# Reordering the end of a step: the next layer norm's logarithm and exponential after the last chunk's reciprocals, and two of chunk 6's normalisation products after chunk 7's mask product

## The chip, the cores and the metric

The kernel runs on one core of a Trainium2 chip, in one launch. The metric is the device time of that launch in microseconds (us), the median of several runs. A core has five engines with an instruction queue each: TensorE (PE, the matrix products; its weight loads are shown as PEld), VectorE (DVE), ScalarE (ACT), GpSimd (POOL) and SyncE (SP, which here only issues the weight transfers).

## The reference, cut to what matters

Four residual blocks, A, B, A, B, on x of 2048 rows by 640 columns, each of the form x + block(layernorm(x)):

```python
def A(x, mem0, Wq, Wk, Wv, Wo):            # 32 heads of 192
    mem = mem0                             # 8 rows
    for s in range(64):                    # segments of 32 rows, one after the other
        h = concat([mem, x[32*s:32*s+32]]) # 40 rows
        q, k, v = h @ Wq, h @ Wk, h @ Wv
        p = softmax(mask(q @ k.T * 192**-0.5))
        o = (p @ v) @ Wo
        mem, out[s] = o[:8], o[8:]

def B(x, wqkv, wo):                        # 32 heads of 20
    # each row attends to 8 earlier rows, 2 apart (itself included)
    return softmax(q @ k_window.T * 20**-0.5) @ v_window @ wo
```

The layer norm is (x - mean) / sqrt(variance + 1e-5), without weights. The memory of A makes its segments a chain. The weights are the same in both A blocks and in both B blocks.

## The kernel before, in words

**Two lanes.** The first A block and the second A block run side by side as two lanes, lane 1 being 3 segments (LAG) behind lane 0: a step t handles segment t in lane 0 and segment t - 3 in lane 1. There are 64 + 3 = 67 steps with A work. In steps 3 to 63 both lanes are full (61 steps, 80 columns: 2 lanes of 8 memory rows and 32 segment rows); in steps 0 to 2 and 64 to 66 only one lane is (40 columns). Block B of a segment runs one and two steps later, cut into pieces that stand between the pieces of A.

**Chunks.** The 32 heads of A are cut into 8 chunks of 4 heads. A chunk has: the projections k, q (`proj`, L220, 30 products each) and v (L249, 10 products); the scores `a_s` (8 products, L267 and L268, into the PSUM tile ps_s; then the exponential E on ScalarE, L270, and its product with a 0/1 mask on VectorE, Em, L273); `a_pv` (8 products of Em with Vt into ps_o, L286; a column block of ones in Vt gives the softmax sums; ScalarE takes their reciprocal R as exp(-ln(sum)): four logarithms, L290, one exponential, L292); `a_norm` (three VectorE products of ps_o with R into OT: L300 for the first and third block of each head pair on all 128 partitions, L301 and L302 for the shared middle block, on partitions 0 to 63 and on 64 to 127); and `a_o` (30 products of OT with Wo, L313, summed over all chunks in ps_acc). `a_o` begins with the 20 products that read what L300 wrote; the last 10 read what L301 and L302 wrote.

**Buffers.** ps_o is two PSUM banks with one buffer (`ps_two`, bufs=1), shared by all chunks: `a_pv` of a chunk may begin once `a_norm` of the chunk before has read ps_o. R, E, Em and QT have one buffer each, OT has two. Four single banks (`ps_big`) go round for the projections, the statistics of the layer norm (ps_st) and block B.

**Weights.** The 64 half-chunks of Wk, Wq, Wv, Wo (480 KB each) are read once per step. 34 of them stay in SBUF; the other 30 go through a ring of 6 buffers (w_ring, L190), each loaded by SP as soon as PE has finished with the buffer.

**Order.** The whole step is under a manual schedule: on each engine the instructions stand in the order in which `step` calls for them, and an engine works its queue in that order, waiting at an instruction until the semaphores that it needs are there.

**The end of a step**, in the order of the code before:

1. `a_k(7)`, `a_q(7)`, `ln1_sq` (square of the next segment's x, L331), `a_pv` of chunk 6, v of chunk 7 and its copies to Vt (L258).
2. `a_norm(6)`: L300, L301, L302 on VectorE.
3. `a_s` of chunk 7: 8 products, E on ScalarE, Em on VectorE. Then `a_o(5)`: 30 products.
4. `ln1(nt)`, the next segment's layer norm: 10 products with ones into ps_st (L339); on VectorE the mean (L346), its square (L348), the variance ln_v (L349); on ScalarE a logarithm (L350) and an exponential (L352), which give 1/sqrt; on VectorE x - mean (L358, which does not read ScalarE's result).
5. `a_pv` of chunk 7 (8 products; four L290 and one L292 on ScalarE), `a_norm(7)` on VectorE, `a_o(6)`: 30 products.
6. `ln1_apply`: two VectorE products (L364) that write the scaled rows to hT.
7. `b_v` and `b_k` of block B: 25 and 30 products (L393) and the ScalarE copies VTB (L410) and KB (L399).
8. `a_o(7)`: 30 products. Then `mem_out` (L327: the memory rows from ps_acc to hT), `b_x1` (L374), `b_q` (30 products) and `b_vt` (5 transposes).

The next step then begins with `a_k(0)`, which reads hT.

Of the kernel before, what the change touches and what calls it, by code (L numbers as in the profile page):

```python
# [60 lines left out]
class Kernel:  # L61
# [230 lines left out]
        nc.scalar.activation(out=rf, in_=rf, func=ACT.Exp, scale=-1.0)  # L292
        self.ov, self.r = ov, r

    def a_norm(self, i):
        nc = self.nc
        ov, r = self.cols(self.ov), self.cols(self.r[:])
        ot = self.ap2.tile([P, 2, 3, NT], BF16, name="OT")
        oc = self.cols(ot[:])
        nc.vector.tensor_tensor(out=oc[:, :, 0:3:2], in0=ov[:, :, 0:4:3], in1=r, op=ALU.mult)  # L300
        nc.vector.tensor_tensor(out=oc[0:64, :, 1], in0=ov[0:64, :, 1], in1=r[0:64, :, 0], op=ALU.mult)  # L301
        nc.vector.tensor_tensor(out=oc[64:P, :, 1], in0=ov[64:P, :, 2], in1=r[64:P, :, 1], op=ALU.mult)  # L302
        self.ots[i] = ot

    def a_o(self, i):
        nc = self.nc
# [35 lines left out]
    def ln_small(self, ps):  # L342

        nc = self.nc
        m = self.ap2.tile([P, NX], F32, name="ln_m")
        nc.vector.tensor_scalar(out=m[:], in0=ps[:, 0:NX], scalar1=1.0 / D, scalar2=None, op0=ALU.mult)  # L346
        v = self.bp.tile([P, NX], F32, name="ln_v")
        nc.vector.tensor_tensor(out=v[:], in0=m[:], in1=m[:], op=ALU.mult)  # L348
        nc.vector.scalar_tensor_tensor(out=v[:], in0=ps[:, NX:2 * NX], scalar=1.0 / D, in1=v[:], op0=ALU.mult, op1=ALU.subtract)  # L349
        nc.scalar.activation(out=v[:], in_=v[:], func=ACT.Ln, bias=self.eps_t[:])  # L350
        r = self.ap2.tile([P, NX], F32, name="ln_r")
        nc.scalar.activation(out=r[:], in_=v[:], func=ACT.Exp, scale=-0.5)  # L352
        return m, r
# [24 lines left out]
        self.bsq = self.ln_sq(x1)  # L378

    def b_ln(self, b):  # L380
        self.bmr = self.ln_small(self.ln_stats(self.x1[b], self.bsq))

    def b_ln_apply(self, b):
        dst = self.h2T[:].rearrange("p c (l n) -> p c l n", l=2)
# [110 lines left out]

    def ln1(self, t):
        x = self.xin[t % 2]
        self.amr = self.ln_small(self.ln_stats(x, self.asq))
        self.axc = self.ln_center(x, self.amr)

    def ln1_apply(self, t):
        self.ln_scale(self.axc, self.amr, self.lanes(self.hT[t % 2][:, 0:NC * NT])[:, :, :, NM:LT])
# [1 line left out]
    def prologue(self):  # L504
        nc = self.nc
        self.x1, self.ots, self.qxs, self.ebs = {}, {}, {}, {}
        self.x_load(0)
        nc.sync.dma_start(out=self.m0T[:], in_=self.mem0)
        nc.vector.tensor_copy(out=self.lanes(self.hT[0][:, 0:NC * NT])[:, :, 0, 0:NM], in_=self.m0T[:])
        self.ln1_sq(0)  # L510
        self.ln1(0)
        self.ln1_apply(0)
        self.build_mask_a()

    def step(self, t):
        T = self.n_seg + LAG
        self.set_lanes(t)
        b1 = t - 1 if 0 <= t - 1 < T else None
        b2 = t - 2 if 0 <= t - 2 < T else None
        nt = t + 1  # L520
        a = t < T
        for i in range(NQUAD - 1):
            if a:
                self.a_k(i, t)
                self.a_q(i, t)
                ps = self.a_v(i, t)
                if i >= 1:
                    self.a_pv()
                self.a_v_out(ps)
                if i >= 2:  # L530
                    self.a_o(i - 2)
            if i == 0 and b1 is not None:
                self.b_ln(b1)
            if b2 is not None and 3 <= i <= 4:
                self.b_pv(i - 3)
            if a and i >= 1:
                self.a_norm(i - 1)
            if b2 is not None and i == 6:
                self.b_wo(b2)
            if b2 is not None:  # L540
                if 1 <= i <= 3:
                    self.b_s(b2, 2 * i - 2)
                    self.b_s(b2, 2 * i - 1)
                if i < 3:
                    self.b_qexp(2 * i)
                    self.b_qexp(2 * i + 1)
                if i == 5:
                    self.b_ot()
            if i == 3 and b1 is not None:
                self.b_ln_apply(b1)  # L550
            if a:
                self.a_s()
            if t == 1 and i in (0, 3):
                self.load_b_weights(i)
            if t == 1 and i == 4:
                self.build_masks_b()
            if i == 1:
                if nt < self.n_seg:
                    self.x_load(nt)
                yseg = t - 3 - LAG  # L560
                if yseg >= 0 and yseg % 4 == 3:
                    self.y_store(yseg // 4)
        if a:
            self.a_k(7, t)
            self.a_q(7, t)
        if nt < T:
            self.ln1_sq(nt)
        if a:
            self.a_pv()
            self.a_v_out(self.a_v(7, t))  # L570
            self.a_norm(6)
            self.a_s()
            self.a_o(5)
        if nt < T:
            self.ln1(nt)
        if a:
            self.a_pv()
            self.a_norm(7)
            self.a_o(6)
        if nt < T:  # L580
            self.ln1_apply(nt)
        if b1 is not None:
            self.b_v(b1)
            self.b_k(b1)
        if a:
            self.a_o(7)
            if nt < T:
                self.mem_out(t)
            self.b_x1(t)
        if b1 is not None:  # L590
            self.b_q(b1)
            self.b_vt()
# [78 lines left out]
```

## Time and profile before

| what | value |
|---|---|
| median of 3 runs | 3419.46 us (3419.04 to 3421.05) |
| the profiled execution | 3423.99 us, of which the profile's span is 3422.3 us |
| granted TensorE clock, mean | 0.99 |
| distance between the memory copies (L327) of two full steps | 50.18 us (in most of them) |
| PE, PEld | 3290.0 us busy (96%), 2885.0 us (84%) |
| DVE, ACT, POOL | 64%, 54%, 11% |
| DMA | 299 GB/s on average |

How to read it: shares are of the span. A row of the timeline gives the start in us from the span's start, the duration in us, the engine, the line, the operation, what it writes and reads, how many equal instructions are merged in it, and in brackets how long the engine had been idle before it and what ended that. Matrix products overlap in the pipeline, so a product's duration is a latency; what counts is the distance between starts (some 0.036 us between products of 80 columns). A line of the waits gives the waiting instruction, what released it, the total in us, how often, and the longest. Durations of VectorE and ScalarE instructions overlap a little too, so that sums are made from starts.

### The profile page before, as it was taken

How to read it: one execution, taken by the hardware profiler on the slowest of the kernel's cores; microseconds unless marked ns; L12 is line 12 of the kernel's file. 1: busy time of each engine (PE TensorE's matmuls, PEld its weight loads, DVE VectorE, ACT ScalarE, POOL GpSimd, SP SyncE). 2: the span in 40 equal slices, each digit the busy share in tenths (PEclk: the TensorE clock that was granted, in tenths of full speed). 3: DMA queues.
4: the chain of work that ended last, by engine and by line, in shares of the span. 5: the costliest groups of instructions: out<-in, count | busy, mean ns of one | idle time of the engine just before them, and what ended most of it. 6: DMA issues, size and time to landing. Idle time of an engine off the chain costs nothing.

```text
span 3422.3 us, 164367 instructions
## 1 busy us (share of the span) xinstructions
PE 3290.0 (96%) x72896; PEld 2885.0 (84%) x72896; DVE 2185.0 (64%) x5966; ACT 1843.2 (54%) x5830; POOL 387.9 (11%) x575
## 2 busy tenths in 40 slices
PE   6899999999999999999999999999999999999996
PEld 4788888888888888888888888888888888888875
DVE  2566666666666666666666666666666666666654
ACT  2455555555555555555555555555555555555543
POOL 0210111011011011101101100110110111011011
PEclk8999999999999999999999999999999999999998
DMA  9988888888888888888888888888888888888894
GB/s 393 349 299 295 307 294 293 307 297 294 298 307 295 293 307 293 296 304 298 294 293 307 295 293 308 292 297 300 302 294 297 308 294 293 310 293 297 296 334 153
DMA packets 298410, 1023.85 MB, mean 299 GB/s; under 512 B 34288, under 2 KB 34288, under 8 KB 297568
## 3 DMA queue, kind: packets, MB, share of 16 engines
q1 hardware_dynamic: 294624, 1004.85, 84.6%
q8 instruction: 570, 9.34, 1.1%
q0 software_dynamic: 3072, 8.48, 0.8%
q14 instruction: 144, 1.18, 0.1%
HBM read 1010.58 MB, written 2.62 MB: 296 GB/s over the span
## 4 chain that ended last, share of the span: by engine, by line
PE 85%; DVE 6%; ACT 4%; DMA 3%; issue 1%; POOL 0%; SPq 0%; POOLq 0%; ACTq 0%
PE ps_v L249 25%; PE ps_k L220 16%; PE ps_q L220 16%; PE ps_acc L313 13%; PE ps_o L286 4%; ACT R L290 2%; PE ps_s L267 2%; PE ps_s L268 2%; PE ps_bq L393 2%; PE ps_bs L433 2%; DVE OT L300 2%; PE ps_by L476 1%; DMA w_ring<-in_A_Wv_dram 1%; DVE Vt L258 1%; ACT R L292 1%
## 5 line engine op out<-in xcount | busy, mean ns | idle before, releaser
L290 ACT ACTIVATE R<-ps_o 64x160 f32<-64x160 f32 (+1 forms) x2144 | 625.4, 292 | 823.8 <-issue 517.3
L258 DVE CAST Vt<-ps_v 80x384 bf16<-80x384 f32 x1072 | 557.9, 550 | 407.9 <-PE ps_o L286 335.5
L249 PEld LDWEIGHTS <-hT 128*128 128x128 bf16 x5360 | 495.3, 99 | 296.6 <-issue 15.6
L425 POOL TENSOR_TENSOR QX<-QB,hmask 128x384 bf16<-128x384 bf16 (+1 forms) x402 | 325.6, 829 | 2844.2 <-ACT QB L404 2204.0
L220 PEld LDWEIGHTS <-w_ring 128*128 128x128 bf16 x15075 | 597.1, 100 | 20.3 <-issue 11.5
L249 PE MATMUL ps_v<-w_ring,hT 128*128 128x384 bf16 x2680 | 532.5, 330 | 5.1 <-DMA w_ring<-in_A_Wv_dram 5.1
L249 PE MATMUL ps_v<-w_v,hT 128*128 128x384 bf16 x2680 | 530.3, 329 | 3.3 <-DMA w_v<-in_A_Wv_dram 3.3
L313 PE MATMUL ps_acc<-OT,w_o 128*128 128x80 bf16 (+1 forms) x9045 | 482.3, 200 | 38.1 <-DVE OT L300 35.9
L300 DVE TENSOR_TENSOR OT<-ps_o,R 128x320 bf16<-128x320 f32 (+1 forms) x536 | 254.3, 475 | 374.4 <-ACT R L292 370.4
L238 DVE CAST QT<-ps_q 128x480 bf16<-128x480 f32 (+1 forms) x536 | 340.2, 635 | 228.6 <-PE ps_q L220 207.4
L313 PEld LDWEIGHTS <-w_o 128*128 128x128 bf16 x9045 | 385.6, 99 | 44.6 <-issue 43.4
L220 PE MATMUL ps_q<-hT,w_q 128*128 128x80 bf16 (+1 forms) x9045 | 405.1, 200 | 5.1 <-DMA w_q<-in_A_Wq_dram 5.1
L313 PE MATMUL ps_acc<-OT,w_ring 128*128 128x80 bf16 (+1 forms) x7035 | 400.0, 200 | 1.5 <-DMA w_ring<-in_A_Wo_dram 1.5
L220 PE MATMUL ps_k<-hT,w_ring 128*128 128x80 bf16 (+1 forms) x8040 | 370.1, 200 | 9.3 <-issue 4.2
L220 PE MATMUL ps_k<-hT,w_k 128*128 128x80 bf16 (+1 forms) x8040 | 369.9, 200 | 4.7 <-issue 2.7
L220 PEld LDWEIGHTS <-w_q 128*128 128x128 bf16 x9045 | 351.0, 100 | 6.1 <-DMA w_q<-in_A_Wq_dram 6.0
L220 PE MATMUL ps_q<-hT,w_ring 128*128 128x80 bf16 (+1 forms) x7035 | 324.4, 200 | 7.7 <-issue 3.9
L220 PEld LDWEIGHTS <-w_k 128*128 128x128 bf16 x8040 | 315.8, 100 | 5.5 <-issue 3.0
L231 ACT CAST KF<-ps_k 128x320 bf16<-128x320 f32 (+1 forms) x536 | 219.5, 409 | 164.7 <-PE ps_k L220 164.1
L313 PEld LDWEIGHTS <-w_ring 128*128 128x128 bf16 x7035 | 306.6, 99 | 1.9 <-DMA w_ring<-in_A_Wo_dram 1.8
L286 PEld LDWEIGHTS <-Vt 80*128 80x128 bf16 x4288 | 208.8, 98 | 81.2 <-DVE Em L273 28.2
L286 PE MATMUL ps_o<-Em,Vt 80*128 80x80 bf16 (+1 forms) x4288 | 239.1, 199 | 20.5 <-DVE Em L273 20.5
(94 smaller groups left out, 4058.1 us busy)
## 6 DMA issues: line engine op xcount, KB each, us to landing
w_ring<-in_A_Wk_dram SPq DMA_DIRECT2D x536, 480.0 KB, 5.1
w_ring<-in_A_Wv_dram SPq DMA_DIRECT2D x536, 480.0 KB, 5.0
w_ring<-in_A_Wq_dram SPq DMA_DIRECT2D x469, 480.0 KB, 4.9
w_ring<-in_A_Wo_dram SPq DMA_DIRECT2D x469, 480.0 KB, 5.3
w_q<-in_A_Wq_dram SPq DMA_DIRECT2D x9, 480.0 KB, 9.6
w_o<-in_A_Wo_dram SPq DMA_DIRECT2D x9, 480.0 KB, 9.6
w_k<-in_A_Wk_dram SPq DMA_DIRECT2D x8, 480.0 KB, 9.6
w_v<-in_A_Wv_dram SPq DMA_DIRECT2D x8, 480.0 KB, 9.8
```

Of the source, the lines that this page charges most:

```text
L220: nc.tensor.matmul(ps[:, NT * n + self.c0:NT * n + self.c1], lhsT=w[:, c, P * (n % 3):P * (n % 3 + 1)], rhs=hT[:, NT * c + self.c0:NT * c ...
L231: nc.scalar.copy(out=kf, in_=pv[:, :, 0:3:2, :])
L238: self.nc.vector.tensor_copy(out=self.cols(qt[:]), in_=self.cols(ps[:, 0:6 * NT].rearrange("p (a n) -> p a n", a=6)))
L249: nc.tensor.matmul(ps[:, 0:384], lhsT=hT[:, NT * c:NT * c + P], rhs=w[:, c, :], start=(c == 0), stop=(c == NC - 1))
L258: self.nc.vector.tensor_copy(out=dst, in_=src)
L267: nc.tensor.matmul(self.cols(sv[:, h]), lhsT=kf[:, NT * h:NT * h + P], rhs=self.cols(qt[:, 3 * pr + 2 * j]), start=True, stop=False)
L268: nc.tensor.matmul(self.cols(sv[:, h]), lhsT=kz[:, NT * h:NT * h + P], rhs=self.cols(qt[:, 3 * pr + 1]), start=False, stop=True)
L286: nc.tensor.matmul(self.cols(ov[:, pr, k]), lhsT=vt[0:NT, 512 * pr + c0:512 * pr + c0 + P], rhs=self.cols(em[0:NT, 2 * pr + k // 2]), star ...
L290: nc.scalar.activation(out=self.cols(r[r0:r0 + 64, :, j]), in_=self.cols(src), func=ACT.Ln)
L300: nc.vector.tensor_tensor(out=oc[:, :, 0:3:2], in0=ov[:, :, 0:4:3], in1=r, op=ALU.mult)
L313: nc.tensor.matmul(self.acc[:, NT * c + self.c0:NT * c + self.c1], lhsT=w[m // 3][:, m % 3, P * c:P * (c + 1)], rhs=self.cols(ot[:, m]), s ...
L425: self.nc.gpsimd.tensor_tensor(out=qx[:, 0:nh, :], in0=self.qb[:, c, :].unsqueeze(1).to_broadcast([P, nh, NX]), in1=self.hmask[:, 0:nh, :] ...
```

## The change

Two things move at the end of a step; nothing is added to or taken from the computation, and the instructions of POOL and SP stay as they are.

`ln1` is cut in two. Its products, its VectorE part and x - mean stay where they were; the logarithm and the exponential on ScalarE (L350 and L352) are issued by `ln1_rstd` after `a_pv` of chunk 7, so that on ScalarE they stand behind the four L290 and the L292 of chunk 7 and ahead of the copies VTB and KB. The layer norm of block B (`b_ln`) keeps its order.

`a_norm(6)` is cut in two. L300 stays in its place; L301 and L302 are issued by `a_norm_mid` after `a_s` of chunk 7, so that on VectorE the order is L300, L273 (Em of chunk 7), L301, L302, where it was L300, L301, L302, L273. All other chunks keep their order.

```diff
-    def a_norm(self, i):
+    def a_norm(self, i, split=False):
         ...
+        self.norm = ov, r, oc
         nc.vector.tensor_tensor(out=oc[:, :, 0:3:2], in0=ov[:, :, 0:4:3], in1=r, op=ALU.mult)
+        self.ots[i] = ot
+        if not split:
+            self.a_norm_mid()
+
+    def a_norm_mid(self):
+
+        nc = self.nc
+        ov, r, oc = self.norm
         nc.vector.tensor_tensor(out=oc[0:64, :, 1], in0=ov[0:64, :, 1], in1=r[0:64, :, 0], op=ALU.mult)
         nc.vector.tensor_tensor(out=oc[64:P, :, 1], in0=ov[64:P, :, 2], in1=r[64:P, :, 1], op=ALU.mult)
-        self.ots[i] = ot
...
         nc.vector.scalar_tensor_tensor(out=v[:], in0=ps[:, NX:2 * NX], scalar=1.0 / D, in1=v[:], op0=ALU.mult, op1=ALU.subtract)
+        return m, v
+
+    def ln_rstd(self, m, v):
+        nc = self.nc
         nc.scalar.activation(out=v[:], in_=v[:], func=ACT.Ln, bias=self.eps_t[:])
         r = self.ap2.tile([P, NX], F32, name="ln_r")
         nc.scalar.activation(out=r[:], in_=v[:], func=ACT.Exp, scale=-0.5)
...
     def b_ln(self, b):
-        self.bmr = self.ln_small(self.ln_stats(self.x1[b], self.bsq))
+        self.bmr = self.ln_rstd(*self.ln_small(self.ln_stats(self.x1[b], self.bsq)))
...
     def ln1(self, t):
         x = self.xin[t % 2]
-        self.amr = self.ln_small(self.ln_stats(x, self.asq))
-        self.axc = self.ln_center(x, self.amr)
+        self.amv = self.ln_small(self.ln_stats(x, self.asq))
+        self.axc = self.ln_center(x, self.amv)
+
+    def ln1_rstd(self):
+        self.amr = self.ln_rstd(*self.amv)
...
             self.a_v_out(self.a_v(7, t))
-            self.a_norm(6)
+            self.a_norm(6, True)
             self.a_s()
+            self.a_norm_mid()
             self.a_o(5)
         if nt < T:
             self.ln1(nt)
         if a:
             self.a_pv()
+        if nt < T:
+            self.ln1_rstd()
+        if a:
             self.a_norm(7)
             self.a_o(6)
```

(The prologue calls `ln1_rstd` right after `ln1`, as before.)

More of the change, by code (lines that the diff above doesn't have):

```diff
@@ L577, in step @@
             self.a_pv()
+        if nt < T:
+            self.ln1_rstd()
+        if a:
             self.a_norm(7)
```

## The prediction

> **What bounds the kernel now.** I read the page first, then PE's waits in the steady part, then the timeline of one end of a step.
>
> ```profile
> PE 3290.0 (96%) x72896; PEld 2885.0 (84%) x72896; DVE 2185.0 (64%) x5966; ACT 1843.2 (54%) x5830; POOL 387.9 (11%) x575
> ```
>
> PE sets the time; only its idle stretches are to be had. The waits of PE between 400 and 3100 us, 54 steps, name all of them:
>
> ```profile
> PE ps_acc L313 <- DVE OT L300: 30.1, 54, 0.6
> PE ps_o L286 <- DVE Em L273: 17.0, 54, 0.3
> PE ps_bq L393 <- issue: 0.9, 2, 0.6
> PE ps_bvt L416 <- issue: 0.2, 1, 0.2
> ```
>
> Two stalls, once per step each: `a_o(7)` waits for L300 of chunk 7, and the second `a_pv` waits for Em of chunk 7. No weight transfer is in the list. The timeline of one step's end, first around the Em stall:
>
> ```profile
> 1532.56 0.43 ACT L270 ACTIVATE E<-ps_s 80x320 bf16<-80x320 f32 x1
> ...
> 1532.75 0.48 DVE L300 TENSOR_TENSOR OT<-ps_o,R 128x320 bf16<-128x320 f32 x1
> ...
> 1533.14 0.31 DVE L301 TENSOR_TENSOR OT<-ps_o,R 64x160 bf16<-64x160 f32 x1
> ...
> 1533.46 0.33 DVE L302 TENSOR_TENSOR OT<-ps_o,R 64x160 bf16<-64x160 f32 x1
> ...
> 1533.82 0.32 DVE L273 TENSOR_TENSOR Em<-E,maskA 80x320 bf16<-80x320 bf16 x1
> 1534.18 0.22 DVE L346 TENSOR_SCALAR ln_m<-ps_st 128x64 f32<-128x64 f32 x1
> 1534.20 0.33 PEld L286 LDWEIGHTS <-Vt 80*128 80x128 bf16 x8 [0.43 <-DVE Em L273]
> ```
>
> E is there at 1532.99, but Em stands behind L301 and L302, ends at 1534.14, and the weight load of L286 follows 0.06 later. Then the other stall:
>
> ```profile
> 1534.95 0.35 ACT L350 ACTIVATE ln_v<-ln_v,eps_t 128x64 f32<-128x64 f32 x1 [1.96 <-DVE ln_v L349]
> 1535.33 0.26 ACT L352 ACTIVATE ln_r<-ln_v 128x64 f32<-128x64 f32 x1
> 1535.60 1.23 ACT L290 ACTIVATE R<-ps_o 64x160 f32<-64x160 f32 x4
> 1536.86 0.47 ACT L292 ACTIVATE R<-R 128x320 f32<-128x320 f32 x1
> 1537.15 0.10 PEld L313 LDWEIGHTS <-w_o 128*128 128x128 bf16 x1
> 1537.23 0.41 ACT L410 CAST VTB<-ps_bv 128x320 bf16<-128x320 f32 x1
> 1537.36 0.49 DVE L300 TENSOR_TENSOR OT<-ps_o,R 128x320 bf16<-128x320 f32 x1 [2.05 <-ACT R L292]
> ...
> 1537.90 0.48 PE L313 MATMUL ps_acc<-OT,w_o 128*128 128x80 bf16 x9 [0.56 <-DVE OT L300]
> ```
>
> ScalarE sits idle for 1.96 us, then serves the layer norm, and only then chunk 7's reciprocals, whose products had begun at 1534.20. PE has its weights for `a_o(7)` at 1537.15 and cannot use them until 1537.90. Unstalled, a product follows its weight load by 0.03 to 0.04 (the loads of `a_o(6)` begin at 1534.46, its products at 1534.50), so it would have begun at 1537.19: the stall costs 0.71 us, more than the 0.56 that is counted from the modelled end of the last product.
>
> **Part 1, the layer norm's two ScalarE instructions.** Elsewhere the first L290 begins 0.49 to 0.54 us after its first L286 product (1525.62 to 1526.11; 1530.15 to 1530.69). Here it takes 1.40. Without L350 and L352 ahead of it: 0.54 (the larger). From the first L290 to L300 it is 1.76, from L300 to the first product 0.54 (both from the rows above). So `a_o(7)` may begin 0.54 + 1.76 + 0.54 = 2.84 us after `a_pv(7)`, and PE gets there after 1537.19 - 1534.20 = 2.99 us. The stall goes whole, 0.71 us, with 0.15 us to spare. The last 10 products need L302, 0.73 + 0.33 us after L300's start: 0.54 + 1.76 + 1.06 = 3.36, against 2.99 + 20 x 0.036 = 3.71.
>
> What is pushed back: L350 and L352 start at 0.54 + 1.26 (four L290) + 0.38 = 2.18 and end near 2.82. L364 reads ln_r, but stands behind L302 and begins at 3.39 at the earliest. VTB behind them on ScalarE begins near 2.9 to 3.0, where it began at 3.03 (1537.23); the idle 1.96 us pays. So this costs nothing. If L352 came late, the next in line would be L327, which waits for the last product of `a_o(7)` in any case (the trace shows it idle for 0.17 us there).
>
> **Part 2, L301 and L302 behind Em.** The waits name Em, but ps_o has one buffer: `a_pv(7)` overwrites what L301 and L302 of chunk 6 read. Before, they stood ahead of Em and the wait for Em covered them. In the changed program's own list of instructions the first weight load of that L286 now waits for the count of chunk 6's last normalisation product, L302's. One wait takes the place of the other, behind the same four VectorE instructions.
>
> What remains is how long the four take in the new order. Old: L300 to L301 0.39, to L302 0.32, to Em 0.36, Em 0.32, to PE 0.06: 1.45. New: L300 to Em 0.40 (E ends 0.16 before that slot, and where Em waits for E it starts 0.04 after E's end, 1546.43 to 1546.47), Em to L301 unknown, L301 to L302 0.32, L302 0.33, to PE 0.06. No row shows Em followed by L301 without a wait. The next rows: Em to L346 0.36, behind L302 to Em 0.36; but L485 (0.32 us long) to Em 0.23, L482 to L485 0.24. The latter two follow 0.08 before the earlier one has ended; the former two wait for an end, and each stands next to L302, which starts at partition 64 (Em behind it; L346 reads PSUM next after it). Em and L301 both start at partition 0, so I take 0.23: 0.40 + 0.23 + 0.32 + 0.33 + 0.06 = 1.34, that is 0.11 us a step gained. With 0.36 it would be 0.02 lost; with the 0.15 from L349 to L358, the closest pair in these rows, 0.19 gained. These are the bounds.
>
> The Trainium skill has a rule for this gap: in "VectorE: DVE Perf Modes", section "Two Vector instructions with no wait between them", an instruction is held until all earlier ones have finished when its input or output starts in another 32-partition quadrant than the last one's. By it L301 behind Em is not held, L302 behind L301 is: the 0.23 case.
>
> Another rule speaks against this half. "Perfetto Trace Analysis", section "Optimization Strategy", says that a gap repeating on the saturated engine can mean too few buffers for the next tile. The waits' row (17.0 us for Em) alone would promise 0.31 us a step; by the rule the buffer is the limit and an order of instructions gives nothing.
>
> **Covers.** POOL and SP keep their order; SP's ring loads come a little earlier, as PE frees buffers. From landings and first uses in steps 10 to 60, a ring half lands 2.5 to 7.7 us (medians by place in the step; least 1.1) before its use, so a step shorter by 0.8 us makes no transfer late; if it did, it would cost what it is late. The granted clock is 1.00 in the steady part and has nothing to give.
>
> **The sum.** 61 full steps x (0.71 + 0.11) = 50.0 us. One-lane steps: in step 64 the products of `a_o(7)` begin 0.56 us late, in step 1 0.37; in steps 2 and 65 PE comes last, step 66 has no layer norm; in step 0 up to 0.9, but the weights are still arriving. Together 0.9 to 1.8, I take 1.2. Gain 51 us. Against the profiled execution: 3424.0 - 51 = 3373 (span 3422.3 to 3371). That execution lies 4.5 us above the median; the gain is idle time per step and carries over as a difference: 3419.5 - 51 = 3368.5 us.
>
> **Rivals.**
> - *Layer norm alone pays*: Em to L301 takes a full 0.36, and the second half gives nothing. 61 x 0.71 + 1.2 = 44.5: 3375 us. For: Em's neighbours at this place do take 0.36; against: those stand beside L302.
> - *Both stalls vanish*: `a_pv(7)` starts as soon as PE is free. PEld's idle time is 0.43, of which 0.11 is in my sum: 61 x 0.32 = 19.5 more, 3349 us. For: the waits name Em alone. Against: the single buffer, and the wait in the program.
> - *Slower*: on VectorE, L301 and L302 now stand behind an Em that waits for E, and `a_pv(7)`, all of chunk 7 and PE stand behind L302. The waits of the whole run have Em waiting for E 71 times, up to 1.2 us. With a wait of 1.16 here, as in a step's first chunk (Em at 1546.47), `a_pv(7)` begins 1.16 later than in my sum: 1.16 - 0.82 = 0.34 lost a step, 61 x 0.34 = 20.7, less 1.2 at the edges: 3439 us. It decides from E 0.12 + 0.82 = 0.94 us later than in this trace; there E is 0.12 early, and nothing ahead of E on ScalarE or PE moves.
> - *The gain does not reach the end*: L290 behind its new wait starts late, or PE meets a new wait of like size in the next step: anything from 3380 to no change.
>
> **How the numbers follow.** Forecast 0.63, layer norm alone 0.20, both stalls 0.04, slower 0.04, partial gain 0.06, no change 0.03. About 0.2% (7 us) is what a measurement of this kernel can tell from no change. The range runs from a second half of 0.19 with 1.8 at the edges (61 x 0.90 + 1.8 = 56.7: 3363) to layer norm alone with 0.02 lost and 0.9 at the edges (61 x 0.69 + 0.9 = 43.0: 3376.5), plus 2.5 if `a_o(7)` still waits 0.04 a step: 3363 to 3379, which holds 0.83. Faster 0.93, same 0.03, slower 0.04.
>
> **What the changed profile would show.** Right: L313 out of PE's waits; the first L290 of chunk 7 some 0.5 us after its L286; L286 waiting for OT of L302 instead of Em, with some 0.3 us of idle weight loads; memory copies 49.36 us apart instead of 50.18. Distances of 49.47 are layer norm alone, 49.0 both stalls. Wrong: a wait of L313 that stays, Em waiting for E, L364 or L327 waiting for ln_r, or DMA among PE's waits.

## The result and the profile after

| | before | changed |
|---|---|---|
| median of the runs | 3419.25 us (3414.13 to 3421.05, 4 runs) | 3381.52 us (3379.19 to 3382.93, 4 runs) |
| ratio, 95% interval | | 0.9891 (0.9874 to 0.9909) |
| the profiled execution, its span | 3423.99, 3422.3 us | 3381.59, 3379.9 us |
| distance of the memory copies of two full steps, undisturbed | 50.18 us | 49.35 us |
| excess: what the 60 distances from step 3 to step 63 are longer than that, in sum | 2.2 us (5 of them over 0.1) | 16.0 us (25 of them over 0.1) |

The kernel became faster by 37.7 us, where 51 were forecast; 3381.5 lies outside the stated 3363 to 3379. The two lines of the table below the span say why: the undisturbed step is within 0.01 us of the forecast 49.36, but many steps are disturbed now.

The page's first part, and the waits of PE between 400 and 3100 us in the changed kernel (engine and line, what released it, total in us, times, longest):

```profile
PE 3277.7 (97%) x72896; PEld 2877.8 (85%) x72896; DVE 2179.0 (64%) x5966; ACT 1845.1 (55%) x5830; POOL 388.5 (11%) x575
```

```profile
PE ps_o L286 <- DVE OT L311: 10.6, 54, 0.2
PE ps_bq L405 <- issue: 5.8, 10, 1.6
PE ps_q L220 <- issue: 2.5, 5, 0.7
PE ps_bvt L428 <- issue: 0.8, 2, 0.7
PE ps_k L220 <- issue: 0.5, 2, 0.4
PE ps_bk L405 <- issue: 0.4, 1, 0.4
PE ps_acc L321 <- issue: 0.4, 1, 0.4
```

The wait of `a_o(7)` (30.1 us before) is gone, and `a_pv(7)` waits for the last normalisation product (L311, the former L302) in place of Em, as forecast. What has grown are the waits for "issue": PE stands still and no semaphore and no other engine explains it. Before there were three of those, 1.1 us in all; here there are 21, 10.4 us in all.

The timeline of one undisturbed end of a step in the changed kernel (L301, L310, L311 are the former L300, L301, L302; L362 and L364 the layer norm's ScalarE instructions; L321 is `a_o`):

```profile
1368.08 0.48 DVE L301 TENSOR_TENSOR OT<-ps_o,R 128x320 bf16<-128x320 f32 x1
...
1368.48 0.31 DVE L273 TENSOR_TENSOR Em<-E,maskA 80x320 bf16<-80x320 bf16 x1
...
1368.71 0.31 DVE L310 TENSOR_TENSOR OT<-ps_o,R 64x160 bf16<-64x160 f32 x1
...
1369.03 0.33 DVE L311 TENSOR_TENSOR OT<-ps_o,R 64x160 bf16<-64x160 f32 x1
...
1369.41 0.33 PEld L286 LDWEIGHTS <-Vt 80*128 80x128 bf16 x8 [0.32 <-DVE OT L311]
...
1369.96 1.23 ACT L290 ACTIVATE R<-ps_o 64x160 f32<-64x160 f32 x4 [1.64 <-PE ps_o L286]
...
1371.60 0.33 ACT L362 ACTIVATE ln_v<-ln_v,eps_t 128x64 f32<-128x64 f32 x1
...
1371.73 0.49 DVE L301 TENSOR_TENSOR OT<-ps_o,R 128x320 bf16<-128x320 f32 x1 [1.19 <-ACT R L292]
...
1372.40 1.24 PE L321 MATMUL ps_acc<-OT,w_o 128*128 128x80 bf16 x30
```

Em to L310 is 0.23 us, from L301's start to the weight load 1.33 (forecast 1.34); the first L290 comes 0.54 after the products began, L301 of chunk 7 2.31 after (2.30), and the 30 products of `a_o(7)` run without an idle stretch.

And a disturbed one, the products of block B's q right behind `a_o(7)`:

```profile
2661.11 0.75 PEld L405 LDWEIGHTS <-wqkv_sb 128*128 128x128 bf16 x23
2661.14 0.84 PE L405 MATMUL ps_bq<-h2T,wqkv_sb 128*128 128x64 bf16 x23
...
2663.57 0.26 PEld L405 LDWEIGHTS <-wqkv_sb 128*128 128x128 bf16 x7 [1.72 <-issue]
2663.57 0.38 PE L405 MATMUL ps_bq<-h2T,wqkv_sb 128*128 128x64 bf16 x7 [1.60 <-issue]
```

PE stops between the 23rd and the 24th of 30 equal products, whose operands have all been there for long. What separates the two is their place in PE's list of instructions (weight loads, products and the semaphore waits among them). Counted there, all 25 stalls over 0.3 us of this kind between 200 and 3250 us stop ahead of instruction 256 n + 194 (or the product right behind its weight load), with n a whole number. The DMA part of the page has a queue that fits (number and kind of the queue, transfers, MB, share of the DMA engines' time; the first is that of the weights):

```profile
q1 hardware_dynamic: 294624, 1004.85, 85.4%
q8 instruction: 570, 9.34, 1.1%
```

570 transfers of 16 KB, for PE's some 146,000 instructions: 256 instructions of 64 bytes in each. In every one of these 25 stalls PE goes on 2.2 to 2.9 us after the start of the last such transfer. These places account for the whole excess: compared product by product over the full steps, every product of the changed kernel that follows the one before it by over 0.05 us more than is usual at its place in the step stands at such a boundary, 31 of them with 15.8 us in sum. So the theory for the experiments: PE runs out of instructions, because at a step's end it works through 256 of them (128 weight loads and products at 0.029 to 0.036 us each, 3.7 to 4.6 us) faster than the next 256 arrive. The rival: the second half of the change, with its new wait ahead of `a_pv(7)`, disturbs something that the profile does not name.

### The profile page after: what moved, and what is told of

It is laid out like the page before. It is cut to its first block, busy times and chain, and to the rows that moved or that the text cites. A ratio compares the mean times of both kernels' runs of the same rounds, so it can differ in the third digit from the quotient of the medians.

```text
span 3379.9 us, 164632 instructions
## 1 busy us (share of the span) xinstructions
PE 3277.7 (97%) x72896; PEld 2877.8 (85%) x72896; DVE 2179.0 (64%) x5966; ACT 1845.1 (55%) x5830; POOL 388.5 (11%) x575
## 4 chain that ended last, share of the span: by engine, by line
PE 91%; DVE 4%; DMA 3%; issue 1%; POOL 0%; ACT 0%; SPq 0%; POOLq 0%; ACTq 0%
PE ps_v L249 25%; PE ps_k L220 16%; PE ps_q L220 16%; PE ps_acc L321 14%; PE ps_o L286 5%; PE ps_s L267 2%; PE ps_s L268 2%; PE ps_bq L405 2%; PE ps_bk L405 2%; PE ps_bs L445 2%; PE ps_bv L405 1%; PE ps_by L488 1%; DMA w_q<-in_A_Wq_dram 1%; DVE Vt L258 1%; DMA w_ring<-in_A_Wq_dram 1%
## 5 line engine op out<-in xcount | busy, mean ns | idle before, releaser
L290 ACT ACTIVATE R<-ps_o 64x160 f32<-64x160 f32 (+1 forms) x2144 | 627.4, 293 | 926.0 <-issue 512.6
L321 PE MATMUL ps_acc<-OT,w_o 128*128 128x80 bf16 (+1 forms) x9045 | 482.5, 200 | 6.6 <-issue 5.2
L301 DVE TENSOR_TENSOR OT<-ps_o,R 128x320 bf16<-128x320 f32 (+1 forms) x536 | 254.7, 475 | 318.3 <-ACT R L292 314.2
L321 PE MATMUL ps_acc<-OT,w_ring 128*128 128x80 bf16 (+1 forms) x7035 | 399.9, 200 | 2.0 <-DMA w_ring<-in_A_Wo_dram 2.0
L321 PEld LDWEIGHTS <-w_o 128*128 128x128 bf16 x9045 | 381.0, 99 | 7.5 <-issue 5.7
L321 PEld LDWEIGHTS <-w_ring 128*128 128x128 bf16 x7035 | 306.6, 99 | 2.3 <-DMA w_ring<-in_A_Wo_dram 2.3
L286 PEld LDWEIGHTS <-Vt 80*128 80x128 bf16 x4288 | 208.9, 98 | 73.4 <-DVE OT L311 20.4
L292 ACT ACTIVATE R<-R 128x320 f32<-128x320 f32 (+1 forms) x536 | 245.7, 458 | 16.9
```

The source lines that it names most:

```text
L286: nc.tensor.matmul(self.cols(ov[:, pr, k]), lhsT=vt[0:NT, 512 * pr + c0:512 * pr + c0 + P], rhs=self.cols(em[0:NT, 2 * pr + k // 2]), star ...
L290: nc.scalar.activation(out=self.cols(r[r0:r0 + 64, :, j]), in_=self.cols(src), func=ACT.Ln)
L321: nc.tensor.matmul(self.acc[:, NT * c + self.c0:NT * c + self.c1], lhsT=w[m // 3][:, m % 3, P * c:P * (c + 1)], rhs=self.cols(ot[:, m]), s ...
```

## The experiments

"Excess" is always the sum defined in the table, "distance" the undisturbed one, both from the experiment's own profile. Each of the kernels is an edit of the changed one.

**The layer norm's half alone.**

```diff
-            self.a_norm(6, True)
+            self.a_norm(6)
             self.a_s()
-            self.a_norm_mid()
```

> Only the layer norm's logarithm and exponential are moved; L300, L301, L302, Em stay in the old order. Theory 'PE's instruction fetch' (with a_o(7) no longer waiting, PE uses up its instructions at the end of a step faster than the 16 KB transfers of the instruction queue bring them, and stands still at every so many instructions): undisturbed full steps 49.47 us apart, and over the 60 distances between full steps an excess of 10 to 20 us above that, as in the changed kernel (16.0; before 2.2); time 3386 to 3392 us. Rival 'the second half disturbs' (the excess comes from L301 and L302 behind Em and the new wait ahead of a_pv(7)): the same 49.47 but an excess of about 2 us; time 3372 to 3378 us.

Measured: 3384.67 us (3382.66 to 3387.27), ratio 0.9903 (0.9888 to 0.9918); distance 49.46, excess 11.4. The excess is within what the theory gave, the time 1.3 us below its range. PE's waits name Em again, and the unexplained ones are there (the first three lines):

```profile
PE ps_o L286 <- DVE Em L273: 16.9, 54, 0.3
PE ps_k L220 <- issue: 3.1, 6, 0.8
PE ps_bq L405 <- issue: 2.4, 4, 1.3
```

The excess does not need the second half: the rival's 2 us is refuted. Whether the second half adds to it (11.4 here, 16.0 and 17.4 with both halves), one trace of the first half alone does not settle.

**The second half alone.**

```diff
             self.ln1(nt)
+            self.ln1_rstd()
         if a:
             self.a_pv()
-        if nt < T:
-            self.ln1_rstd()
```

> Only L301 and L302 of chunk 6 are moved behind Em; the layer norm's two ScalarE instructions stay ahead of chunk 7's reciprocals, so that a_o(7) still waits 0.7 us in each step. Theory 'PE's instruction fetch': undisturbed steps 50.07 us apart (0.11 less than before), an excess of 1 to 5 us, since the stall ahead of a_o(7) still gives the fetch time; 3410 to 3414 us. Rival 'the second half disturbs': the excess of some 14 us shows here; 3422 to 3427 us. If Em to L301 took 0.36, the distance would be 50.20.

Measured: 3411.40 us (3408.25 to 3416.23, 10 runs), ratio 0.9982 (0.9972 to 0.9992); distance 50.07, excess 3.7. The reordering on VectorE is worth 0.11 us a step, and while `a_o(7)` waits in each step there is little excess:

```profile
PE ps_acc L321 <- DVE OT L301: 30.0, 54, 0.6
```

**The changed kernel again, on the same chip.**

> The changed kernel once more, beside the two halves on the same chip. Both theories: 49.35 us between undisturbed steps, excess 12 to 20 us, 3379 to 3384 us; the stalls again at the same places in PE's stream of instructions, but of other lengths.

Measured: 3381.50 us (3374.14 to 3382.78); distance 49.35, excess 17.4.

**Without the weight stream.** What is left out: from step 1 on the 30 ring halves of a step are not loaded; others of the same kind stand in for them.

```diff
         res = key in self.resident
+        if not res and self.t > 0:
+            return self.units[next(u for u in self.resident_list if u[0] == kind)]
```

> The changed kernel without the weight stream: from step 1 on every half-chunk that went through the ring uses a half of the same kind that stays in SBUF (other numbers, the same instructions on PE but for one semaphore wait per step), so that after step 0 hardly anything but instructions, x and the result goes through the DMA engines. Theory 'the fetch is late because its transfers share the DMA engines with the weights': no stalls of PE that nothing explains, excess under 3 us, and the time from the start of an instruction transfer to the first use of it in a stall, 2.2 to 2.5 us, or the delay before its start, clearly shorter. Rival 'the fetch is asked for too late, whatever the load': stalls at the same places and an excess of 8 to 20 us. Undisturbed steps 49.35 us apart under both.

Measured: distance 49.35, excess 0.03: all 60 distances are the same to within 0.1 us. 3336.56 us in its one run, which also saves weight loading in the first steps and is not to be compared as a time. Its whole list of PE's waits between 400 and 3100 us (L290 and L315 there are L286 and L311 of the changed kernel), and two of its queues:

```profile
PE ps_o L290 <- DVE OT L315: 10.9, 55, 0.2
```

```profile
q1 hardware_dynamic: 9504, 31.51, 2.4%
q8 instruction: 570, 9.34, 1.2%
```

The same 570 instruction transfers, the same products, and no unexplained stall. From the first use of a block of 256 instructions (instruction 256 n + 194) to the start of the transfer of the next, between 200 and 3250 us, it takes 1.6 us (median; a quarter take over 2.0) with the stream and 0.2 (a quarter over 0.3) without. The transfers themselves are not shorter without the stream, 1.09 us (median) against 0.97. So the transfers of instructions start late because of the weight stream; that the request itself comes too late whatever the load, the rival, is refuted.

**With half the weight stream.** Left out: the ring halves of v and of Wo from step 1 on.

```diff
-        if not res and self.t > 0:
+        if not res and self.t > 0 and kind in "vo":
```

> The changed kernel with half of the weight stream: from step 1 on the ring halves of v and of Wo are replaced by halves that stay in SBUF (other numbers), those of k and q are still loaded, 15 in place of 30 per step. Theory 'the fetch waits for its turn behind weight transfers': excess 0 to 5 us, and the delay from the first use of one block of 256 instructions to the start of the transfer of the next between the 2.0 us (median) of the full stream and the 0.3 us of none. Rival 'any stream at all does it': excess over 10 us.

Measured: distance 49.35, excess 0.03; the delay of the transfers is 0.3 us (median; a quarter take over 0.7), between those of the full stream and of none. The 2.0 and 0.3 us that the expectation calls medians are the bounds of those slowest quarters. The weights' queue carries half of its bytes, and all queues together 161 GB/s instead of 303:

```profile
q1 hardware_dynamic: 152064, 518.18, 47.3%
```

With half the traffic nothing of the stalls is left.

**The place of the boundary.** If blocks of 256 are what counts, it must matter where in the step a block ends. The changed kernel has 2180 PE instructions per full step, so that the boundaries drift through all places. With 2176, which is 8.5 blocks, they stay at two sets of places, in alternate steps.

```diff
     def b_ln(self, b):
-        ... self.ln_stats(self.x1[b], self.bsq) ...      # 10 products of 64 columns
+        ... self.ln_stats2(self.bboth) ...               # 5 products of 128: x1 and its square in one tile
     def ln1(self, t):
-        ... self.ln_stats(x, self.asq) ...
+        ... self.ln_stats(x, self.asq, 3 if t > 1 else 11) ...   # first so many products of one column
```

> The changed kernel with exactly 2176 instructions per full step on PE (8.5 transfers of 256): block B's mean and square sums come from 5 products of 128 columns in place of 10 of 64 (x1 and its square in one tile), and 3 products of one column are added ahead of the layer norm's statistics in `ln1`, where PE then waits for a_pv(7) in any case. 11 such products in each of the first two calls set the place of the boundaries: in one step at instruction 14 of the step, in the next 114 instructions before the step's end, where the changed kernel's trace shows stalls of 0 to 0.1 us. Theory 'PE's instruction fetch': undisturbed steps 49.30 to 49.40 us apart, excess 0 to 6 us, 3365 to 3371 us. Rival 'the stalls come from load alone, wherever the boundary is': excess 12 to 20 us, 3379 to 3384 us.

Measured: 3374.73 us (3372.06 to 3376.95), ratio 0.9866 (0.9850 to 0.9883); distance 49.33, excess 10.5. The same with 19 in place of 11:

> The same kernel with 19 in place of 11 one-column products in each of the first two calls (16 products more in the whole run, some 0.5 us): the boundaries stand at instruction 110 of one step and 18 before the end of the next, where the changed kernel's trace shows stalls of 0.1 to 0.8 and 0.5 to 1.8 us. Theory 'PE's instruction fetch': excess 25 to 50 us in every second step's end, 3390 to 3415 us. Rival 'load alone, wherever the boundary is': no difference from the kernel with 11, within 3 us.

Measured: 3388.02 us (3383.75 to 3389.03), ratio 0.9904 (0.9890 to 0.9919); distance 49.33, excess 26.3. The idle weight loads of PE between 400 and 3100 us, first with 11, then with 19 (L416 is block B's products there, L321 `a_o`):

```profile
PEld L286 <- DVE OT L311: 13.2, 55, 0.2
PEld L220 <- issue: 6.8, 10, 1.6
PEld L321 <- issue: 2.0, 4, 1.1
```

```profile
PEld L416 <- issue: 18.5, 27, 1.3
PEld L286 <- DVE OT L311: 12.9, 54, 0.2
PEld L220 <- issue: 2.6, 5, 0.7
```

With 19 the excess lies within its range, the time 2 us below it. Sixteen products of one column at the very start of the run cost 13.3 us at its end. With 19, the boundary 19 instructions before a step's end stalls in 29 of 30 passes, 0.67 us on average; the boundary in the middle of a step does so almost never in either kernel. "Load alone, wherever the boundary is" is refuted by the difference. My sizes were off: with 11 I had expected an excess of at most 6 and a time of at most 3371 us, from places that the changed kernel's trace had passed only a few times each; the place 13 instructions into the step stalls in 11 of 30 passes, by 0.20 on average.

**A ring of 5 weight buffers.**

```diff
-RING = 6
+RING = 5
```

> The changed kernel with a ring of 5 in place of 6 weight buffers: the same bytes, but one transfer fewer outstanding at a time; PE's instructions stand at the same places as in the changed kernel. If the fetch waits behind whatever is outstanding: excess 5 to 12 us in place of 16 to 17. If it is the rate alone: 14 to 20 us. Weights land some 1.7 us later relative to their use, so PE may wait for some of them: up to 10 us more.

Measured: 3395.65 us in one run; excess 25.0, of which the waits for weights are 1.3 us in the window above. Of the excess some 21.6 us stand at the block boundaries and 2.9 elsewhere, all of that ahead of products with weights from the ring. Neither expectation held: one transfer fewer outstanding did not help the instructions. The delay before their transfers start is hardly changed, 1.65 us (median) against 1.58. Why the stalls grew stays open.

**The boundary at the best place found.**

```diff
-        ... self.ln_stats(x, self.asq, 3 if t > 1 else 11) ...
+        ... self.ln_stats(x, self.asq, 3 if t > 1 else 2) ...
```

> The kernel with 2176 PE instructions per step again, with 2 one-column products in each of the first two calls: the boundaries stand at instruction 49 of one step and 79 before the end of the next, where the stalls of five traces taken together (the changed kernel twice, the layer norm alone, boundaries with 11 and 19) average 0.0. At 13 and 115 before the end they averaged 0.20 and 0.09, at 109 and 19 before the end 0.11 and 0.67. Theory 'PE's instruction fetch, decided by where the boundary falls': 49.33 us between undisturbed steps, excess 0 to 5 us, 3364 to 3370 us. Rival 'the place only shifts the stalls about': excess 9 to 16 us, 3373 to 3381 us.

Measured: 3373.05 us (3369.11 to 3374.30), ratio 0.9862 (0.9845 to 0.9878); distance 49.33, excess 7.2. The boundary 79 before a step's end stalls in 10 of 30 passes (0.19 on average), the one at 49 in 3 (0.04). Again more than hoped: the excess lies between the ranges of the theory and of the rival, and the time at the lower edge of the rival's, so this run does not decide between them. Nor can the kernel be told from the one with 11 (excess 10.5) by the times. But it has the lowest median of the complete kernels here, 46 us under the kernel before in its own session and some 8.5 under the changed one, across sessions.

## Why the prediction was wrong, point by point

*Layer norm.* Right: forecast 0.71 us a step, measured 50.18 - 49.46 = 0.72 with this half alone. Each of the links (0.54, 1.76, the start of L350 at 2.18) came within 0.02 us.

*L301 and L302 behind Em.* Right in both parts: the wait for the single ps_o buffer takes the place of the wait for Em (10.6 us in PE's list, 17.0 before), and the order on VectorE brings 50.18 - 50.07 = 0.11, forecast 0.11. Em to L310 is 0.23, not 0.36. The rule that the prediction cites from the Trainium skill, "VectorE: DVE Perf Modes", section "Two Vector instructions with no wait between them", gave the same 0.23 for a pair that the trace before did not show, and the trace after agrees with it. That the single buffer leaves an order of instructions nothing to gain was too strong: of the 0.31 us a step in the waits' row the order took 0.11, and 0.20 stay.

*The step that failed: "Covers".* There I named the ring's weight transfers and the granted clock as what could be late next, and gave a step shortened by 0.8 us no further cost. Weights are indeed not late: no wait for one appears in PE's list after. What is late is PE's own instructions, a term that the sum put at nothing. Over 60 distances the undisturbed gain is 60 x 0.835 = 50.1 us, and 16.0 - 2.2 = 13.8 of it is given back as excess. With the excess of before, the 3381.5 would have been some 3368. Of the rivals, "the gain does not reach the end" came true in kind (PE meets a new wait, at the end of the step or in the next one), though the wait is not of like size: 13.8 us over 60 distances is 0.23 a step. I had priced it at 3380 and more and given it 0.06; the range ended at 3379.

The signs were in the profile before, and I passed over both. I quoted "PE ps_bq L393 <- issue: 0.9, 2, 0.6" as part of the complete list of waits and asked nothing about it; the instruction stream's own line stands in the page's DMA part. In the trace before, the few stalls of this kind already stop ahead of instruction 256 n + 194. The delay of the transfers was the same then (median 1.5 us, a quarter over 2.0), but with a wait of 0.7 us in each step, right where PE is fastest, no block between 200 and 3250 us was used up in less than 4.4 us. Without the weight stream, where PE does not stall, the quickest blocks of the new order take 3.6. In none of these traces does PE begin a block sooner than 2.2 us after the start of its transfer; a delay of 2.0 and these 2.2 are covered by 4.4 us and not by 3.6.

The Trainium skill, in "Runtime: NRT & Kernel Launch", section "Instruction fetch mechanics", says that instructions are refilled in 16 KiB blocks of 256 by a DMA queue of the engine's own while the current block is worked on, and that crossing a boundary is mostly hidden. The runs agree with the blocks; that the cost is hidden, they show only where PE is slower or the DMA engines are less busy: 2.2 us of excess in the kernel before, 0.03 in the changed one without the weight stream, but 16 to 17 with it, and 26 with the boundary at a bad place. The Trainium skill, in "DMA: Bandwidth & Descriptors", section "Queues, rings and completion order", has each DMA engine take its queues in turn, a packet at a time; that would make a transfer of instructions wait for weight packets, and fits the order of the delays, 0.2, 0.3 and 1.6 us (medians) with none, half and all of the stream. The turn-taking itself is not seen in these runs.

*The edges.* Forecast 1.2 us, with a 61st full step 2.0. The two spans differ by 42.4, so some 6 us lie in the first and last steps. Across the traces with the full weight stream the start up to step 3's copy varies from 229.7 to 234.1 us and the part behind step 63's from 168.7 to 175.3 (the trace before had 233.9 and 175.3), so this term can't be resolved.

*What stays open.* Why five ring buffers make the stalls worse, and how far a weight stream ordered around the end of a step would bring the excess down; the latter was not tried.

## What to carry to other kernels

When the busiest engine is nearly full, ask of a removed wait not only which operand is late next, but whether the engine's instructions are: count them per microsecond in the densest stretch, look for idle time that nothing explains ("issue") in the trace before, and see whether it falls every 256 instructions. Many small matrix products in a row beside a heavy weight stream are where it shows. A change then has two results, the step that is forecast and the place at which the block boundaries fall; compare variants by their undisturbed step first, and only then by their times.

## What the runs showed of the hardware that was not expected

- PE's instructions come in transfers of 256 (16 KB), 570 in this kernel. Where it had run out in the changed kernel, PE went on 2.2 to 2.9 us after the start of the last transfer (up to 3.4 with the layer norm's half alone). The transfer itself takes 0.97 of that (median); what the rest is, no run shows.
- The start of such a transfer comes 0.2 us after PE's first use of the block before it when the DMA engines carry no weights, 0.3 us at 161 GB/s, and 1.6 us at 303 GB/s (medians; a quarter come after more than 0.3, 0.7 and 2.0 us).
- Sixteen tiny products more at the start changed the time of a 3.4 ms kernel by 13 us, by shifting the boundaries.
- One buffer fewer for the weights, at the same rate (302 GB/s), did not make the instructions come earlier (1.65 us).
